# Linear attention and a gated MLP on one core: the second batch's keys loaded earlier and in pieces, the z products in quarters of the array, the last output in halves

## The chip, the cores and the metric

The kernel runs on one core of one Trainium2 chip. The metric is the device time of one execution in microseconds (us), the median of several runs. The core has TensorE (PE, its weight loads shown as PEld), VectorE (DVE), ScalarE (ACT), GpSimd (POOL) and SyncE (SP), which here only issues DMAs. SBUF has 128 partitions, and TensorE writes to PSUM.

## The reference

```python
def _attn_ref(q, k, v, S1, S2):          # q, k, v: 4 batches, 4 heads, 1088 rows, 32 columns; S1, S2: 8 x 32
    def phi(x):
        a = np.einsum('rd,bhsd->bhsr', S1, x)
        b = np.einsum('rd,bhsd->bhsr', S2, x)
        return np.einsum('bhsi,bhsj->bhsij', a, b).reshape(*x.shape[:-1], r * r)   # 64 features
    q_p, k_p = (phi(q), phi(k))
    kv = np.einsum('bhsf,bhsd->bhfd', k_p, v)
    z = np.sum(k_p, axis=2)
    num = np.einsum('bhsf,bhfd->bhsd', q_p, kv)
    den = np.einsum('bhsf,bhf->bhs', q_p, z)[..., None] + 1e-06
    return num / den

def _moe_ref(x, w_gate, w_val, w_out, rms_g):   # x: 4352 rows of 128; 128 x 1536, 128 x 1536, 1536 x 128
    xn = x / np.sqrt(np.mean(x * x, axis=-1, keepdims=True) + 1e-06) * rms_g
    g = xn @ w_gate
    return g * (1.0 / (1.0 + np.exp(-g))) * (xn @ w_val) @ w_out
```

The attention's output, with its heads side by side, is the input x of the gated MLP.

## The kernel before

**Tiling.** The 4352 rows are taken in nine chunks: eight of 512 columns and one of 256. The 1536 hidden columns are twelve slices j of 128. One pair of chunk and slice is a slot, 108 in all: three matmuls for the gate (`g_ps`), three for the value (`v_ps`), a Silu on ACT (`s`), a product on DVE (`h`), and one to three matmuls that add into `o_ps`. Three matmuls stand for one fp32 product, because operands are split into a rounded part and a rest (`w_hi`, `w_lo`, `x_hi`, `x_lo`, `h_hi`, `h_lo`). The first two chunks run slices 0 to 5 and then 6 to 11.

**Weights.** A slice arrives as raw double-precision words (`w_raw`, 384 KB). ACT takes the absolute value (`w_tmp`), DVE makes fp32 of it in four steps (L310, L315, L320, L324), ACT and POOL split it. This goes on until about 57 us, beside the first slots.

**Keys.** `kside` handles one batch of keys: a load of `kt` and of `vt` in pieces, matmuls with `s_t` (L482) that give both projections a and b, copies of these to `ab` by ACT (`bring`, L509), their outer product `phi`, then the sums over the rows. Batch 0 has its own path at the start. For batches 1 to 3 `kv_turned` forms kv by 36 small matmuls (L407) and z by nine products of a and b over 128 rows each (L401): a 64 x 32 result that holds all heads against all heads. ACT copies it to `gram`, and four matmuls with the constant `spread` and a mask `column` pick the wanted entries out of it.

**Queries.** `qside` divides by den, takes squares (`sq`), a root on POOL (`rstd`), scales (`xn`), transposes on TensorE (L764), and makes `x_hi` (ACT) and `x_lo` (DVE). For chunk 0 this is done for rows 0 to 255 and 256 to 511 apart; the first half's squares are DVE's and the second half's are ACT's.

**Order.** A planner (`Plan.run`) walks all tasks with assumed costs, keys (due times) and clocks for each engine, and writes each engine's instructions out in the order it finds; the engines then run them strictly in that order. Where it expects TensorE to idle early on, it puts in fillers (`keep_warm`, L292), matmuls of zeros into an `att` bank of PSUM. Every `keep_warm` is one matmul, and one fp32 matmul shows as two records in the trace. `att` has three banks; the fillers' tile holds one of them until the last filler. Keys of batch 1 go into two `att` banks (`ahead`) during the prologue, and TensorE can write such a bank only when its earlier reader is done. SP's loads take eight semaphores in turn, and each load waits for the landing of the one eight places ahead.

**What the change touches.** `K1` holds the four due times of batch 1's `kside` (its key matmuls, its outer products, its sums, its loads). The last slot's output is copied in two halves of 128 columns, by ACT and by DVE, into one tile `o_sb`, and goes out by one DMA of SP.

## Time and profile before

| | us |
|---|---|
| median of 3 runs (lowest to highest) | 270.78 (270.42 to 270.82) |
| the profiled execution's own time | 270.91 |
| its span, first to last instruction | 269.1 |
| busy: PE | 262.6 (98%) |
| busy: DVE | 189.5 (70%) |
| busy: ACT | 153.2 (57%) |
| busy: POOL | 66.7 (25%) |

The profiled execution took 270.91 us, of which 1.81 us lie outside the span. Times in the rows are counted from the span's start. A row of the timeline gives start, duration, engine, line, operation, what is written from what, count, and in brackets how long the engine was idle before and what released it. "issue" there means that no single cause shows.

### The profile page before, as it was taken

How to read it: one execution, taken by the hardware profiler on the slowest of the kernel's cores; microseconds unless marked ns; L12 is line 12 of the kernel's file. 1: busy time of each engine (PE TensorE's matmuls, PEld its weight loads, DVE VectorE, ACT ScalarE, POOL GpSimd, SP SyncE). 2: the span in 40 equal slices, each digit the busy share in tenths (PEclk: the TensorE clock that was granted, in tenths of full speed). 3: DMA queues.
4: the chain of work that ended last, by engine and by line, in shares of the span. 5: the costliest groups of instructions: out<-in, count | busy, mean ns of one | idle time of the engine just before them, and what ended most of it. 6: DMA issues, size and time to landing. Idle time of an engine off the chain costs nothing.

```text
span 269.1 us, 5080 instructions
## 1 busy us (share of the span) xinstructions
PE 262.6 (98%) x1899; PEld 208.9 (78%) x1899; DVE 189.5 (70%) x378; ACT 153.2 (57%) x319; POOL 66.7 (25%) x79
## 2 busy tenths in 40 slices
PE   8889999999999999999999999999999999999995
PEld 5758677677887878878887887788887888788894
DVE  5769999666847887677666795678568566766532
ACT  4457763675654544565556554565655565665662
POOL 3033751367350130001800220003300700100262
PEclk9979999999999999999999999999999999999999
DMA  6999500642521520035002500024002200100010
GB/s 202 363 388 371 181 2 0 200 110 58 130 67 48 153 57 2 1 100 131 26 0 80 148 11 2 0 85 130 4 0 68 61 0 0 40 2 0 0 41 21
DMA packets 12953, 22.11 MB, mean 82 GB/s; under 512 B 1664, under 2 KB 5760, under 8 KB 12928
## 3 DMA queue, kind: packets, MB, share of 16 engines
q1 hardware_dynamic: 12928, 21.78, 25.8%
q8 instruction: 15, 0.25, 0.4%
q14 instruction: 10, 0.08, 0.1%
HBM read 18.69 MB, written 3.08 MB: 81 GB/s over the span
## 4 chain that ended last, share of the span: by engine, by line
PE 96%; DMA 2%; issue 1%; SPq 0%; DVE 0%; ACT 0%
PE g_ps L822 27%; PE v_ps L822 27%; PE o_ps L853 23%; PE o_ps L840 4%; PE att L659 4%; DMA q<-qT 2%; PE att L764 2%; PE att L482 2%; PE att L401 1%; PE att L407 1%; PE att L675 1%; PE o_ps L531 1%; PE att L572 1%; PE att L292 1%; PE att L591 0%
## 5 line engine op out<-in xcount | busy, mean ns | idle before, releaser
L833 DVE TENSOR_TENSOR h<-v_ps,s 128x512 f32<-128x512 f32 (+2 forms) x109 | 71.1, 654 | 28.1 <-PE v_ps L822 12.1
L242 ACT CAST h_hi<-h 128x512 fp32r<-128x512 f32 (+1 forms) x91 | 54.2, 596 | 52.5 <-DVE h L833 52.3
L829 ACT ACTIVATE s<-g_ps 128x512 f32<-128x512 f32 (+1 forms) x108 | 62.0, 574 | 25.1 <-PE g_ps L822 22.5
L250 DVE TENSOR_TENSOR h_lo<-h,h_hi 128x512 fp32r<-128x512 f32 x74 | 53.0, 720 | 32.0 <-ACT h_hi L242 31.0
L822 PE MATMUL g_ps<-x_hi,w_hi 128*128 128x512 f32 (+1 forms) x110 | 46.0, 419 | 0.0
L822 PE MATMUL v_ps<-x_hi,w_hi 128*128 128x512 f32 (+1 forms) x110 | 42.2, 383 | 0.0
L822 PE MATMUL g_ps<-x_hi,w_lo 128*128 128x512 f32 (+1 forms) x110 | 42.0, 382 | 0.0
L822 PE MATMUL g_ps<-x_lo,w_hi 128*128 128x512 f32 (+1 forms) x110 | 41.7, 379 | 0.0
L822 PE MATMUL v_ps<-x_hi,w_lo 128*128 128x512 f32 (+1 forms) x110 | 41.5, 377 | 0.0
L822 PE MATMUL v_ps<-x_lo,w_hi 128*128 128x512 f32 (+1 forms) x110 | 41.4, 377 | 0.0
L757 POOL TENSOR_TENSOR rstd<-ms,mhalf 128x4 f32<-128x4 f32 (+1 forms) x10 | 9.5, 951 | 112.3 <-DVE ms L773 111.9
L853 PE MATMUL o_ps<-h_hi,w_lo 128*128 128x512 f32 (+1 forms) x94 | 36.1, 384 | 0.0
L853 PE MATMUL o_ps<-h_hi,w_hi 128*128 128x512 f32 (+1 forms) x94 | 36.1, 384 | 0.0
L853 PE MATMUL o_ps<-h_lo,w_hi 128*128 128x512 f32 (+1 forms) x94 | 36.0, 383 | 0.0
L249 POOL TENSOR_TENSOR h_lo<-h,h_hi 128x512 fp32r<-128x512 f32 (+1 forms) x20 | 20.4, 1029 | 30.7 <-ACT h_hi L242 30.6
L822 PEld LDWEIGHTS g_ps<-x_hi,w_hi 128*128 128x128 f32 x110 | 20.7, 188 | 6.5 <-issue 1.8
L822 PEld LDWEIGHTS g_ps<-x_hi,w_lo 128*128 128x128 f32 x110 | 20.7, 188 | 5.0 <-issue 1.7
L822 PEld LDWEIGHTS v_ps<-x_hi,w_hi 128*128 128x128 f32 x110 | 20.7, 188 | 4.6 <-DVE ms L773 0.2
L249 POOL TENSOR_TENSOR w_lo<-w_f,w_hi 128x256 fp32r<-128x256 f32 (+1 forms) x24 | 17.2, 734 | 28.2 <-ACT w_hi L242 28.1
L822 PEld LDWEIGHTS g_ps<-x_lo,w_hi 128*128 128x128 f32 x110 | 20.9, 190 | 4.2
L822 PEld LDWEIGHTS v_ps<-x_hi,w_lo 128*128 128x128 f32 x110 | 20.7, 188 | 4.1 <-issue 0.2
L822 PEld LDWEIGHTS v_ps<-x_lo,w_hi 128*128 128x128 f32 x110 | 20.6, 188 | 4.0
(104 smaller groups left out, 301.3 us busy)
## 6 DMA issues: line engine op xcount, KB each, us to landing
w_raw<-w SPq DMA_DIRECT2D x12, 384.0 KB
at<-far SPq DMA_DIRECT2D x12, 256.0 KB
bt<-far SPq DMA_DIRECT2D x24, 128.0 KB
q<-qT SPq DMA_DIRECT2D x8, 256.0 KB
outT<-o_sb SPq DMA_DIRECT2D x8, 256.0 KB
vt<-v SPq DMA_DIRECT2D x9, 204.0 KB
kt<-kT SPq DMA_DIRECT2D x9, 192.0 KB
far<-abt SPq DMA_DIRECT2D x12, 64.0 KB
```

Source lines behind the costliest of these rows:

```text
L242: "act": (n * 0.835 + 172, lambda: nc.scalar.copy(out=out(), in_=in_()), 0),
L249: "pool": (n * 2.1 + 150, lambda: nc.gpsimd.tensor_tensor(out=out(), in0=in_(), in1=hi(), op=ALU.subtract), 0),
L250: "dve": (n * 1.04 + 140, lambda: nc.vector.tensor_tensor(out=out(), in0=in_(), in1=hi(), op=ALU.subtract), penalty, True),
L482: nc.tensor.matmul(out=abv[hf * HALF:(hf + 1) * HALF, t - t0, :], lhsT=kt()[:, s0:s0 + HALF], rhs=sblk_t, start=True, stop=True)
L659: nc.tensor.matmul(out=nv[hf * HALF:(hf + 1) * HALF, t, p, :], lhsT=phiqs[c][1]()[:, p, l0:l0 + HALF], rhs=kvs[(STARTS[c] + l0) // S][:, p ...
L757: nc.gpsimd.tensor_tensor(out=rstd()[:, us, 0], in0=ms()[:, us], in1=mhalf[:, us], op=ALU.pow)
L764: nc.tensor.transpose(out=xt()[:, t * P:(t + 1) * P], in_=xn()[:, t, :], identity=ident)
L822: nc.tensor.matmul(out=acc()[:, cs], lhsT=wt[:, j, i3, :], rhs=x()[:, cs], start=(i == 0), stop=(i == 2))
L829: act(n, t + 0.3, lambda: nc.scalar.activation(out=s()[:, :n], in_=gps()[:, :n], func=AF.Silu), cols(gps, whole[0]), [s])
L833: lambda cs=cs: nc.vector.tensor_tensor(out=h()[:, cs], in0=vps()[:, cs], in1=s()[:, cs], op=ALU.mult),
L840: lambda cs=cs: nc.tensor.matmul(out=o_ps()[:, cs], lhsT=w_f[:, j, 2], rhs=h()[:, cs], start=first, stop=last and cs.stop == n),
L853: nc.tensor.matmul(out=o_ps()[:, :n], lhsT=wt[:, j, 2, :], rhs=x()[:, :n], start=first and i == 0, stop=last and i == 2,)
```

## The change

- `K1`'s load time goes from -26.5 to -28.2, and batch 1's values get load times of their own, `VT1` = (-15, -14, -13). On SP's queue the three key pieces then stand ahead of the second weight slice, and the three value pieces behind the eighth.
- The keys of a batch in `ahead` (batch 1) become three planner tasks, one for each piece of three tiles of 128 rows, where one task waited for all three pieces. ACT's three copies wait for their own piece.
- z's nine products (L401): the 64-column operand that held both a and b becomes a's 32 columns, and the product of tile t goes to quarter t % 4 of the output's partitions. The four quarters are summed later by the matmuls with `spread`, which now has 128 rows in place of 64; `gram` is 128 x 32. For this `ab` is laid out with all of a ahead of all of b.
- `spread` and `column` are made on POOL by six instructions, ahead of the four memsets of `kv`, where DVE made them by five. The planner's clock for POOL starts at 5200 in place of 2200.
- The last output's halves have tiles of their own (`o_end0`, `o_end1`), and each goes out by its own DMA: ACT's half on ACT's queue, DVE's half on SP's.

```diff
-K1 = -41,9,10,-26.5
+K1 = -41,9,10,-28.2
+VT1 = (-15, -14, -13)
...
-    spread = const.tile([NB, H, F], F32, name="spread")
-    for h in range(H):
-        nc.vector.tensor_copy(
...
-    nc.vector.tensor_reduce(out=column, in_=ident.rearrange("p (o j) -> p j o", j=R), axis=AX.X, op=ALU.add)
+    spread = const.tile([P, H, F], F32, name="spread")
+    column = const.tile([P, 4 * R], F32, name="column")
+
+    def patterns():
+        nc.gpsimd.tensor_tensor(out=column, in0=ident[:, :4 * R], in1=ident[:, 4 * R:8 * R], op=ALU.add)
+        for k in (2, 3):
+            nc.gpsimd.tensor_tensor(out=column, in0=column, in1=ident[:, 4 * k * R:4 * (k + 1) * R], op=ALU.add)
+        nc.gpsimd.tensor_copy(
+            out=spread.rearrange("p h (i j) -> p (h i) j", j=R), in_=column.unsqueeze(2).to_broadcast([P, H * R, R])
+        )
+        for k in (2, 1):
+            nc.gpsimd.tensor_tensor(out=column[:, :k * R], in0=column[:, :k * R], in1=column[:, k * R:2 * k * R], op=ALU.add)
+
+    patterns()
...
             for t in range(KT):
-                ab = abs_[t // 3]()[:, t % 3]
-                nc.tensor.matmul(
-                    out=tr()[:NB, :H * R], lhsT=ab.rearrange("p h c r -> p (h c r)"), rhs=ab[:, :, 1, :], start=(t == 0), stop=(t == KT - 1)
-                )
+                a, b = (abs_[t // 3]()[:, c, t % 3].rearrange("p h r -> p (h r)") for c in range(2))
+                rows = slice(t % 4 * H * R, (t % 4 + 1) * H * R)
+                nc.tensor.matmul(out=tr()[rows, :H * R], lhsT=a, rhs=b, start=(t < 4), stop=(t >= KT - 4), skip_group_check=True)
...
-        act(H * R, key, lambda: nc.scalar.copy(out=gram(), in_=tr()[:NB, :H * R]), [tr], [gram])
+        act(H * R, key, lambda: nc.scalar.copy(out=gram(), in_=tr()[:, :H * R]), [tr], [gram])
...
-    ktl, vtl = early if first else ([early] * 3, (early + 0.5, early + 2, early + 2))
+    ktl, vtl = early if first else ([early] * 3, (early + 0.5, early + 2, early + 2) if b > 1 else VT1)
...
-        abs_ = [sb("ab", [P, 3, H, 2, R], 3) for _ in groups]
+        abs_ = [sb("ab", [P, 2, 3, H, R], 3) for _ in groups]
...
-        if not first:
+        if b in ahead:
+            for g, (lo, hi) in enumerate(pieces):
+                pe(453, kab, lambda lo=lo, hi=hi, g=g: mm(lo, hi, banks[g // 2], g // 2 * 6), [(kt, g), "sblk"], [(banks[g // 2], g)], True)
+        elif not first:
             pe(151 * KT, kab, mms, [(kt, g) for g in range(3)] + ["sblk"], banks, True)
...
+        if not left:
+            for i, cs in enumerate(rest_of):
+                o_end, wd = sb(f"o_end{i}", [P, P], 1), cs.stop - cs.start
+                if i:
+                    dve(wd * 1.04, t + 1.0, lambda cs=cs, o=o_end: nc.vector.tensor_copy(out=o(), in_=o_ps()[:, cs]), done, [o_end])
+                else:
+                    act(wd, t + 1.0, lambda cs=cs, o=o_end: nc.scalar.copy(out=o(), in_=o_ps()[:, cs]), done, [o_end])
+                load(
+                    wd * P * 4, t, lambda cs=cs, o=o_end, on=nc.sync if i else nc.scalar: on.dma_start(
+                        out=out[:, s0 + cs.start:s0 + cs.stop], in_=o()
+                    ), [("out", c, i)], [o_end],
+                )
+            return
...
-    plan.run({"pe": PE0, "act": 1900, "dve": 1000, "pool": 2200, "dma": 600}, keep_warm, SLOW, URGENT, WINDOW)
+    plan.run({"pe": PE0, "act": 1900, "dve": 1000, "pool": 5200, "dma": 600}, keep_warm, SLOW, URGENT, WINDOW)
```

The planner moves instructions that the diff does not name. The line numbers grow by seven to ten in the prologue's tasks, so L482, L292, L764, L822, L330, L739, L509, L787 and L780 of before are L489, L300, L774, L832, L338, L749, L519, L797 and L790 of the changed kernel.

SP's queue in the prologue, from the gain vector on, before: kt are keys (192 KB a piece), vt values, w_raw weight slices, q queries.

```order
L884 DMA gain_t<-gain 128x1
L383 DMA w_raw<-w 128x768
L465 DMA kt<-kT 128x384 x3
L383 DMA w_raw<-w 128x768
L468 DMA vt<-v 128x408
L552 DMA q<-qT 128x512
L468 DMA vt<-v 128x408 x2
L383 DMA w_raw<-w 128x768 x2
```

The same stretch now:

```order
L901 DMA gain_t<-gain 128x1
L472 DMA kt<-kT 128x384 x3
L391 DMA w_raw<-w 128x768 x2
L562 DMA q<-qT 128x512
L391 DMA w_raw<-w 128x768 x2
L562 DMA q<-qT 128x512
```

The second weight slice stands behind the three key pieces, and the value pieces have left the stretch.

ACT's order in the prologue, from the second half of chunk 0's phi (phiq) to x_hi of the first half, before. The first w_tmp row is slice 1's, the second slice 2's; sq are the squares of the second half of chunk 0's rows; the three ab rows are batch 1's.

```order
L605 COPY phiq_228<-v_ps_234 128x2x256
L330 ACTIVATE w_tmp_255<-w_raw_184 128x384
L242 CAST w_hi_98<-w_f_100 128x256
L242 CAST w_hi_98<-w_f_100 128x128
L330 ACTIVATE w_tmp_309<-w_raw_232 128x384
L739 ACTIVATE sq_317,ss_318<-x_274 128x128 x2
L509 COPY ab_324<-att_281 128x192
L509 COPY ab_328<-att_281 128x192
L509 COPY ab_335<-att_294 128x192
L787 ACTIVATE x_hi_340<-att_332,gain_t_97 128x256
```

The same stretch now:

```order
L615 COPY phiq_230<-v_ps_235 128x2x256
L243 CAST w_hi_99<-w_f_101 128x256
L243 CAST w_hi_99<-w_f_101 128x128
L338 ACTIVATE w_tmp_289<-w_raw_214 128x384
L519 COPY ab_302<-att_271 128x12x2x8
L519 COPY ab_309<-att_271 128x12x2x8
L519 COPY ab_318<-att_294 128x12x2x8
L338 ACTIVATE w_tmp_323<-w_raw_233 128x384
L749 ACTIVATE sq_327,ss_328<-x_280 128x128 x2
L797 ACTIVATE x_hi_344<-att_338,gain_t_98 128x256
```

The three copies of batch 1's keys and slice 2's w_tmp have moved ahead of the squares.

TensorE from batch 1's keys to the first matmuls of slot 0, before:

```order
L482 MATMUL att<-s_t,kt 64x64 x18
L292 MATMUL att<-const-float32-0.0 1x128 x2
L764 MATMUL att<-ident,xn 128x128 x2
L292 MATMUL att<-const-float32-0.0 1x128 x2
L764 MATMUL att<-ident,xn 128x128 x2
L572 MATMUL att<-s_t,q 128x64 x2
L822 MATMUL g_ps<-x_hi,w_hi 128x256
```

The same stretch now:

```order
L489 MATMUL att<-s_t,kt 64x64 x18
L300 MATMUL att<-const-float32-0.0 1x128 x5
L774 MATMUL att<-ident,xn 128x128 x2
L300 MATMUL att<-const-float32-0.0 1x128 x2
L832 MATMUL g_ps<-x_hi,w_hi 128x256
```

Five fillers stand between the keys and the first transposes in place of two, and the first half's gate matmuls (three, of which the last row is the first) have moved ahead of the second half's transposes. The order of the 108 slots behind it is the same.

More of the change, by code (lines that the diff above doesn't have):

```diff
@@ L259, in attention_then_glu @@
     nc.vector.memset(ones, 1.0)
-    spread = const.tile([NB, H, F], F32, name="spread")
-    for h in range(H):
-        nc.vector.tensor_copy(
-            out=spread[:, h].rearrange("p (i j) -> p i j", j=R),
-            in_=ident[:NB, 2 * h * R:(2 * h + 1) * R].unsqueeze(2).to_broadcast([NB, R, R]),
-        )
-    column = const.tile([P, R], F32, name="column")
-    nc.vector.tensor_reduce(out=column, in_=ident.rearrange("p (o j) -> p j o", j=R), axis=AX.X, op=ALU.add)
+    spread = const.tile([P, H, F], F32, name="spread")
[6 more added lines that the diff above has]
+            out=spread.rearrange("p h (i j) -> p (h i) j", j=R), in_=column.unsqueeze(2).to_broadcast([P, H * R, R])
+        )
+        for k in (2, 1):
+            nc.gpsimd.tensor_tensor(out=column[:, :k * R], in0=column[:, :k * R], in1=column[:, k * R:2 * k * R], op=ALU.add)
+    patterns()
     zeros = nc.const_aps.tensor(0.0, [P, P], F32)
@@ L395, in kv_turned @@
         acc, tr = ps("att", 3), ps("att", 3)
-        both, gram, picked = sb("kv_both", [P, 2, F], 1), sb("gram", [NB, H * R], 1), sb("picked", [P, 2, R], 1)
+        both, gram, picked = sb("kv_both", [P, 2, F], 1), sb("gram", [P, H * R], 1), sb("picked", [P, 2, R], 1)
         def kvmm():
             for t in range(KT):
-                ab = abs_[t // 3]()[:, t % 3]
-                nc.tensor.matmul(
-                    out=tr()[:NB, :H * R], lhsT=ab.rearrange("p h c r -> p (h c r)"), rhs=ab[:, :, 1, :], start=(t == 0), stop=(t == KT - 1)
-                )
+                a, b = (abs_[t // 3]()[:, c, t % 3].rearrange("p h r -> p (h r)") for c in range(2))
+                rows = slice(t % 4 * H * R, (t % 4 + 1) * H * R)
+                nc.tensor.matmul(out=tr()[rows, :H * R], lhsT=a, rhs=b, start=(t < 4), stop=(t >= KT - 4), skip_group_check=True)
             for t in range(KT):
@@ L412, in kv_turned @@
         pe(
-            1450, key, kvmm, [(phis[g], g) for g in range(3)] + [(vt, g) for g in range(3)] + [(abs_[g], g) for g in range(3)],
+            1330, key, kvmm, [(phis[g], g) for g in range(3)] + [(vt, g) for g in range(3)] + [(abs_[g], g) for g in range(3)],
             [acc, tr], True,
         )
-        act(H * R, key, lambda: nc.scalar.copy(out=gram(), in_=tr()[:NB, :H * R]), [tr], [gram])
+        act(H * R, key, lambda: nc.scalar.copy(out=gram(), in_=tr()[:, :H * R]), [tr], [gram])
         act(
@@ L437, in kv_turned @@
             17, key, lambda: nc.vector.tensor_tensor(
-                out=picked(), in0=sums(), in1=column.unsqueeze(1).to_broadcast([P, 2, R]), op=ALU.mult
+                out=picked(), in0=sums(), in1=column[:, :R].unsqueeze(1).to_broadcast([P, 2, R]), op=ALU.mult
             ), [tr], [picked],
@@ L498, in outer @@
             def outer(eng, ab=ab, phi=phi, ts=ts, m=m, near=near, ab_ps=ab_ps, o=o):
-                both = ab()[:, ts].rearrange("p t h c r -> p (t h) c r")
+                both = ab()[:, :, ts].rearrange("p c t h r -> p (t h) c r")
                 a = ab_ps()[:, o:o + m * HALF].rearrange("p (th c r) -> p th c r", c=2, r=R) if near else both
@@ L509, in bring @@
                 nc.scalar.copy(
-                    out=ab()[:, ts].rearrange("p t h c r -> p (t h) c r")[:, :, c0:],
+                    out=ab()[:, :, ts].rearrange("p c t h r -> p (t h) c r")[:, :, c0:],
                     in_=ab_ps()[:, o:o + m * HALF].rearrange("p (th c r) -> p th c r", c=2, r=R)[:, :, c0:],
@@ L515, in kside @@
                 pe(151 * m, kab, lambda lo=lo, hi=hi, ab_ps=ab_ps: mm(lo, hi, ab_ps, lo), [(kt, g), "sblk"], [ab_ps], True)
-            act(HALF * m // (2 if first and near else 1), kab, bring, [ab_ps], [(ab, i)])
+            act(HALF * m // (2 if first and near else 1), kab, bring, [(ab_ps, g) if b in ahead else ab_ps], [(ab, i)])
             if near or b in SBD:
@@ L873, in slot @@
         else:
-            for i, cs in enumerate(rest_of):
-                if i:
-                    dve(
-                        (cs.stop - cs.start) * 1.04, t + 1.0,
-                        lambda cs=cs: nc.vector.tensor_copy(out=o_sb()[:, cs], in_=o_ps()[:, cs]), done, cols(o_sb, cs),
-                    )
-                else:
-                    act(cs.stop - cs.start, t + 1.0, lambda cs=cs: nc.scalar.copy(out=o_sb()[:, cs], in_=o_ps()[:, cs]), done, cols(o_sb, cs))
+            act(n, t + 1.0, lambda: nc.scalar.copy(out=o_sb()[:, :n], in_=o_ps()[:, :n]), done, cols(o_sb, whole[0]))
         load(n * P * 4, t, lambda: nc.sync.dma_start(out=out[:, s0:s0 + n], in_=o_sb()[:, :n]), [("out", c)], cols(o_sb, whole[0]))
```

## Prediction

> **What bounds the kernel now.** I read the page's busy times and the chain that ended last, then the stretches of the prologue, then its timeline, since the change touches three places: the prologue, the z products and the last output.
>
> ```profile
> PE 262.6 (98%) x1899; PEld 208.9 (78%) x1899; DVE 189.5 (70%) x378; ACT 153.2 (57%) x319; POOL 66.7 (25%) x79
> ...
> PE 96%; DMA 2%; issue 1%; SPq 0%; DVE 0%; ACT 0%
> ```
>
> TensorE is busy for 98% of the span and makes 96% of the chain. So microseconds taken from TensorE's own work after the prologue count in full, and work of other engines counts only where TensorE waits for it. That is in the prologue:
>
> ```profile
> 12.20:15.60 3.40, 1.64 (x47) 1.42 (x46) 3.16 (x14) 1.66 (x6) 1.44 (x2) 1.00 1.05 392
> 15.60:19.00 3.40, 3.40 (x24) 1.66 (x21) 1.49 (x5) 2.13 (x10) 1.17 (x2) 0.51 1.01 383
> ```
>
> The columns are length, busy time of PE, PEld, DVE, ACT and POOL with counts, TensorE's granted clock, DMA share and GB/s. From 12.2 to 15.6 us TensorE works 1.64 of 3.40 us; from 15.6 to 19.0 it has about half its clock (0.51). Between 19.46, the first row of slot 0, and the tail I find no wait in its timeline.
>
> ```profile
> 11.81 1.84 SPq L383 DMA_DIRECT2D w_raw<-w  x2
> ...
> 13.39 0.43 DVE L715 TENSOR_TENSOR x<-att,rden 128x256 f32<-128x256 f32 x1
> ...
> 13.77 0.36 SPq L552 DMA_DIRECT2D q<-qT  x1
> ...
> 13.92 0.92 PE L482 MATMUL att<-s_t,kt 128*64 128x64 f32 x24 [1.20 <-issue]
> ...
> 14.51 0.55 ACT L330 ACTIVATE w_tmp<-w_raw 128x384 f32<-128x384 f32 x1 [0.95 <-DMA w_raw<-w]
> ...
> 14.88 0.42 DVE L715 TENSOR_TENSOR x<-att,rden 128x256 f32<-128x256 f32 x1
> ...
> 15.22 0.35 DVE L310 TENSOR_SCALAR w_tmp<-w_tmp 128x384 f32<-128x384 f32 x1
> ...
> 15.34 0.31 ACT L739 ACTIVATE sq<-x 128x128 f32<-128x128 f32 x1 [0.28 <-DVE x L715]
> ...
> 15.40 0.73 PE L482 MATMUL att<-s_t,kt 128*64 128x64 f32 x12 [0.57 <-PE att L482]
> ...
> 15.94 0.74 ACT L509 COPY ab<-att 128x192 f32<-128x192 f32 x3
> ...
> 16.06 1.01 PE L292 MATMUL att<-const-float32-0.0 128*1 128x128 f32 x4
> ...
> 16.31 0.74 POOL L757 TENSOR_TENSOR rstd<-ms,mhalf 128x2 f32<-128x2 f32 x1 [0.99 <-DVE ms L773]
> ...
> 17.01 0.69 PE L764 MATMUL att<-ident,xn 128*128 128x128 f32 x2
> ...
> 17.73 0.47 ACT L787 ACTIVATE x_hi<-att,gain_t 128x256 fp32r<-128x256 f32 x1 [1.06 <-PE att L764]
> 18.10 0.68 ACT L780 ACTIVATE xn<-x,rstd 128x128 f32<-128x128 f32 x2
> 18.24 0.48 DVE L767 SCALAR_TENSOR_TENSOR x_lo<-att,gain_t,x_hi 128x256 fp32r<-128x256 f32 x1 [1.75 <-ACT x_hi L787]
> ...
> 19.46 0.37 PE L822 MATMUL g_ps<-x_hi,w_hi 128*128 128x256 f32 x1
> ...
> 19.97 0.48 DVE L767 SCALAR_TENSOR_TENSOR x_lo<-att,gain_t,x_hi 128x256 fp32r<-128x256 f32 x1
> ```
>
> **Keys loaded earlier: nothing.** The key matmuls start at 13.92, 0.10 us after DVE ends x (13.39 + 0.43 = 13.82), and go on at 15.40, 0.10 after the second x (15.30). These x read the `att` banks into which the keys go: with one bank held by the fillers' tile, only two are left. The keys had landed: the two weight loads at 11.81 to 13.65 and the query load at 13.77 stand eight places behind the three key pieces and waited for them. So the transfer taken forward is not what TensorE waits for. DVE's order up to both x is unchanged but for the patterns (below), so 13.92 and 15.40 stay.
>
> **The second weight slice later: nothing.** It swaps places with the key pieces, so it lands at the latest when the third of them did, 13.77. ACT's w_tmp takes 0.55 and DVE's next step on it starts at 15.22: 0.9 us of cover. Without it, x_lo behind that DVE step would be late by what is missing. The values are needed only by the kv products, quoted below, long after slot 0's start, and the later slices land earlier.
>
> **ACT's new order and five fillers: 0 to 1.4 us lost, 1.1 taken.** Before, the key matmuls end about 16.1, two fillers (four records) take 16.06 to 17.01, 0.24 a record, and the transposes of the first half follow. Now ten records follow: 16.06 + 10 x 0.24 = 18.43 at half clock, 1.42 late. The chain behind it is x_hi 0.72 later (19.15), x_lo 0.51 after that (19.66), then DVE's same three weight steps, and x_lo of the second half 1.73 after the first (21.39 to 21.87, before 20.45). ACT's side comes in time for that: its third key copy waits for the keys (about 16.15), then a copy of 0.25, w_tmp of 0.55 and squares of 0.60 (15.34 to 15.94) end near 17.5 instead of 15.94; rstd then ends near 18.5 instead of 17.05, ahead of x_hi at 19.15. So the squares' delay of 1.5 us hides under the fillers. If the fillers ran at full clock, half the time each, they would end at 16.06 + 1.2 = 17.3 and x_hi would wait for the squares at 17.5: no later than 17.73. The lower end is therefore 0, the upper 1.4. I take 1.1, near the row's half clock, less something because the slow stretch need not fall on all ten records in each run. [...]
>
> **z in quarters: 2.6 us gained.** The z products and the kv products of one batch, and the same pair later, in the chain:
>
> ```profile
> 44.31 1.17 PE att L401 x18
> 45.47 1.14 PE att L407 x72
> ...
> 101.05 1.17 PE att L401 x18
> 102.21 1.14 PE att L407 x72
> ...
> 160.08 1.16 PE att L401 x18
> 161.25 1.14 PE att L407 x72
> ```
>
> L401 has 18 records in 1.17 us, 65 ns each: a 64-column operand, always at the same columns of the array. L407 has 72 in 1.14, 16 ns each: 32 columns, in turn on four quarters. The changed products have L407's shape, with 32 moving columns instead of 64, and the same turn. At 16 ns they take 18 x 0.016 = 0.29, so 0.88 less, and I take 0.86, three times: 2.6. The other end: the key matmuls, two halves of the array in turn, have 24 records in 0.92 us, 38 ns, which gives 0.69 and a gain of 0.48, 1.4 in all. L407 is the nearer row. With the change of shape between L401 and L407 gone, up to 0.1 more each. [...]
>
> `spread` with 128 rows instead of 64, and ACT's copy of 128 instead of 64 partitions: eight records and one copy as before, so nothing; ends -0.1 and +0.1 for all three. ACT's key copies now write in strides: no row has that at this size, so 0 to 0.1.
>
> **Patterns on POOL: nothing.**
>
> ```profile
> 1.25 0.66 POOL L273 MEMSET kv<- 128x132 f32 x4
> ...
> 2.66 0.20 DVE L338 TENSOR_SCALAR s_low<-s_raw 128x64 uint32<-128x64 uint32 x1 [0.25 <-DMA s_raw<-sw]
> ...
> 5.80 1.07 POOL L501 TENSOR_TENSOR phi<-ab 128x512 f32<-128x512 f32 x1 [3.89 <-ACT ab L509]
> ...
> 7.76 1.59 PE L531 MATMUL o_ps<-vt,phi 128*64 128x34 f32 x48
> ```
>
> DVE loses five instructions but then waits for s_raw until 2.66, so it gains nothing. POOL idles 3.89 us ahead of phi, which TensorE reads in the second third of L531's row, about 8.3, 1.4 us after phi's end at 6.87. So 5.3 us are covered.
>
> ```profile
> L249 POOL TENSOR_TENSOR w_lo<-w_f,w_hi 128x256 fp32r<-128x256 f32 x12 | 10.7, 893 | 24.9 <-ACT w_hi L242 24.9
> ...
> L249 POOL TENSOR_TENSOR w_lo<-w_f,w_hi 128x128 fp32r<-128x128 f32 x12 | 6.9, 574 | 3.3 <-ACT w_hi L242 3.2
> ```
>
> Five small sums at no more than 0.57 and one copy of 256 columns at no more than 0.89 are 3.8 us. Above 5.3 each further microsecond would be one of the whole.
>
> **The last output: 0.3 us gained.**
>
> ```profile
> 265.81 0.27 ACT L881 COPY o_sb<-o_ps 128x128 f32<-128x128 f32 x1 [1.34 <-PE o_ps L840]
> 266.11 0.29 DVE L878 COPY o_sb<-o_ps 128x128 f32<-128x128 f32 x1 [1.06 <-ACT o_sb L881]
> 266.43 0.33 SPq L882 DMA_DIRECT2D outT<-o_sb  x1
> ```
>
> DVE's copy waits for ACT's, and the DMA for both. With tiles apart both copies can start at 265.81, and both DMAs issue near 266.13: 0.30 less. A first DMA on ACT's queue has no row; SP's issues took 0.33 here and 1.84 for two above, so between -0.3 and +0.3.
>
> **Sum.** 270.91 - 2.6 - 0.3 + 1.1 = 269.1 for the profiled execution. It lies 0.13 above the median of 270.78, so against the runs shown: 269.0.
>
> **Rivals.** First, the fillers cost nothing, because the slow stretch falls elsewhere: 270.78 - 2.9 = 267.9. For it speaks that the fillers then end before the squares do; against it the 0.51 of the row that covers them. Second, the quarters overlap only as the halves of the key matmuls do, 38 ns: 270.78 - 1.4 - 0.3 + 1.1 = 270.2. Third, on the other side: the z products stay at 65 ns each, because the spacing comes from issuing and not from the array. Then nothing pays for the prologue: 270.78 - 0.3 + 1.1 = 271.6. It decides from about 50 ns a record, where the gain of 3 x 18 x 15 ns = 0.8 only pays the rest. L407's 16 ns is against it. Fourth, the slow stretch lasts for another 3.4 us, since the idle time ahead of it is as before and more of it is filled with zeros: half of 3.4, 1.7 us more, 270.7, no change. Against it: the two stretches above, where full work in one was followed by full clock at 19.46.
>
> **How the numbers follow.** Forecast 0.60, first rival 0.18, second 0.09, third 0.07, fourth 0.06. A measurement of this kernel can tell about 0.2%, 0.54 us, from no change: faster means below 270.24. Faster are the forecast, the first rival and half of the second: 0.60 + 0.18 + 0.045, rounded to 0.82. Same are the fourth and the other half: 0.11. Slower is the third: 0.07. The range from 267.8 to 270.4 holds the forecast, the first rival and most of the second; the forecast alone, with the prologue between 0.6 and 1.4 and the tail between 0 and 0.35, lies within 268.4 to 269.6.
>
> **What would show it.** z: eighteen records of L410 in about 0.3 us, and L414 straight behind. Prologue: the keys (L489) still at 13.9 and 15.4, ten filler records behind them, the first transposes (L774) near 18.4 instead of 17.0, squares (L749) near 16.9, the last gate rows of slot 0 near 22 instead of 20.5. Patterns: phi on POOL still near 5.8. Tail: both copies at once, the DMAs 0.3 us behind the first. The forecast is wrong if L410 keeps more than 40 ns a record, if the half clock misses the fillers or stays past 19.5, or if TensorE waits anywhere behind slot 0.

## The result, and the profile after

The changed kernel takes 267.69 us (median of 4 runs, 267.10 to 267.80), the kernel before 270.60 in the same comparison (median of 4, 270.20 to 270.82): a ratio of 0.989, interval 0.987 to 0.9909. That is 1.1% faster, and just below the range of the prediction. Timed again beside other kernels, the changed kernel took 267.78 (6 runs, 267.49 to 269.45) against 270.15 (11 runs, 269.85 to 271.06): 0.9922, interval 0.9899 to 0.9945. Why the two ratios differ is part of what follows.

The profiled execution took 267.65 us, with a span of 265.9 (before 269.1). From its page, and from its view by stretches, the rows that answer to those of before:

```profile
PE 260.1 (98%) x1905; PEld 206.6 (78%) x1905; DVE 189.9 (71%) x373; ACT 153.0 (58%) x319; POOL 68.4 (26%) x85
```

```profile
12.20:15.60 3.40, 1.63 (x48) 1.41 (x46) 3.16 (x14) 1.59 (x5) 1.44 (x2) 1.00 1.02 402
15.60:19.00 3.40, 3.35 (x29) 1.95 (x25) 1.65 (x5) 2.47 (x9) 1.16 (x2) 1.00 1.03 408
```

TensorE is idle for as long as before in the first stretch (busy 1.63 of 3.40 us), but the second one, which had a clock of 0.51, now has 1.00. This is the first surprise. The timeline of the prologue shows what that did:

```profile
13.79 0.92 PE L489 MATMUL att<-s_t,kt 128*64 128x64 f32 x24 [1.20 <-issue]
...
15.29 0.57 PE L489 MATMUL att<-s_t,kt 128*64 128x64 f32 x12 [0.58 <-PE att L489]
...
15.79 1.27 PE L300 MATMUL att<-const-float32-0.0 128*1 128x128 f32 x10
...
16.61 0.30 ACT L749 ACTIVATE sq<-x 128x128 f32<-128x128 f32 x1
...
16.99 0.44 PE L774 MATMUL att<-ident,xn 128*128 128x128 f32 x2
...
17.46 0.47 ACT L797 ACTIVATE x_hi<-att,gain_t 128x256 fp32r<-128x256 f32 x1 [0.17 <-PE att L774]
```

The keys start at 13.79 and 15.29, ten filler records follow, and ScalarE's squares come at 16.6: all close to the forecast. But the ten records take 1.27 us and not 2.4, so the first transposes stand at 16.99 (before 17.01) and not at 18.4.

The z products and what stands around them, in TensorE's timeline before and after (L675 and L685 are the first instruction behind the pair of z and kv products):

```profile
44.24 1.24 PE L401 MATMUL att<-ab 128*64 128x32 f32 x18
45.40 1.21 PE L407 MATMUL att<-phi,vt 128*32 128x64 f32 x72
46.54 0.66 PE L675 MATMUL att<-q,sab 128*64 128x128 f32 x8
```

```profile
44.28 0.34 PE L410 MATMUL att<-ab 128*32 128x32 f32 x17
44.43 0.26 PE L414 MATMUL att<-phi,vt 128*32 128x64 f32 x3
44.46 0.20 PE L410 MATMUL att<-ab 128*32 128x32 f32 x1
44.49 1.17 PE L414 MATMUL att<-phi,vt 128*32 128x64 f32 x69
45.59 0.66 PE L685 MATMUL att<-q,sab 128*64 128x128 f32 x8
```

The pair starts 0.04 us later than before (so the new prologue as a whole gained nothing in these two executions, although only the one before has a half-clock stretch) and takes 45.59 - 44.28 = 1.31 us instead of 46.54 - 44.24 = 2.30. The other two pairs gain the same. The kv products' first row stands 0.15 behind the first z product: 17 of the 18 records have started by then, the last starts 0.03 later.

The tail, its last products before, and then what the changed kernel has:

```profile
264.73 1.04 PE L840 MATMUL o_ps<-h,w_f 128*128 128x256 f32 x6
```

```profile
261.73 1.04 PE L850 MATMUL o_ps<-h,w_f 128*128 128x256 f32 x6
262.81 0.27 ACT L883 COPY o_end<-o_ps 128x128 f32<-128x128 f32 x1 [1.32 <-PE o_ps L850]
263.10 0.37 ACTq L885 DMA_DIRECT2D outT<-o_end  x1
263.10 0.29 DVE L881 COPY o_end<-o_ps 128x128 f32<-128x128 f32 x1 [1.04 <-ACT o_end L883]
263.42 0.33 SPq L885 DMA_DIRECT2D outT<-o_end  x1
```

From the end of the last product (262.77) to the end of the span (265.87) it is 3.10 us, before 265.77 to 269.10, 3.33: 0.23 gained. But VectorE's copy still waits for ScalarE's, although the tiles they write are now apart, so the last DMA is issued no earlier: 0.65 behind the last product, before 0.66 (the prediction has that row, 266.43). What is shorter is the time from that issue to the end of the span, 2.45 instead of 2.67; that DMA now carries one half instead of both.

So from profile to profile: three pairs at 0.99 to 1.00, 3.0; the tail 0.23; the prologue 0. That is the 3.2 us between the two spans.

### The profile page after: what moved, and what is told of

It reads as the page before. It is cut to its first block, busy times and chain, and to the rows that moved or that the text cites. A ratio compares the mean times of both kernels' runs of the same rounds, so it can differ in the third digit from the quotient of the medians.

```text
span 265.9 us, 5091 instructions
## 1 busy us (share of the span) xinstructions
PE 260.1 (98%) x1905; PEld 206.6 (78%) x1905; DVE 189.9 (71%) x373; ACT 153.0 (58%) x319; POOL 68.4 (26%) x85
## 4 chain that ended last, share of the span: by engine, by line
PE 98%; issue 1%; DVE 0%; ACT 0%
PE g_ps L832 28%; PE v_ps L832 27%; PE o_ps L863 23%; PE o_ps L850 4%; PE att L669 4%; PE att L300 2%; PE att L774 2%; PE att L489 1%; PE att L414 1%; PE att L685 1%; PE o_ps L541 1%; PE att L582 1%; PE g_ps L489 0%; PE att L601 0%; PE v_ps L489 0%
## 5 line engine op out<-in xcount | busy, mean ns | idle before, releaser
L832 PE MATMUL g_ps<-x_hi,w_hi 128*128 128x512 f32 (+1 forms) x110 | 46.1, 419 | 0.0
L832 PE MATMUL v_ps<-x_hi,w_hi 128*128 128x512 f32 (+1 forms) x110 | 42.3, 384 | 0.0
L832 PE MATMUL g_ps<-x_hi,w_lo 128*128 128x512 f32 (+1 forms) x110 | 42.0, 381 | 0.0
L832 PE MATMUL g_ps<-x_lo,w_hi 128*128 128x512 f32 (+1 forms) x110 | 41.7, 379 | 0.0
L832 PE MATMUL v_ps<-x_lo,w_hi 128*128 128x512 f32 (+1 forms) x110 | 41.5, 378 | 0.0
L832 PE MATMUL v_ps<-x_hi,w_lo 128*128 128x512 f32 (+1 forms) x110 | 41.5, 377 | 0.0
L832 PEld LDWEIGHTS g_ps<-x_hi,w_hi 128*128 128x128 f32 x110 | 20.7, 188 | 6.8 <-issue 1.8
L832 PEld LDWEIGHTS g_ps<-x_hi,w_lo 128*128 128x128 f32 x110 | 20.7, 188 | 5.0 <-issue 1.7
L832 PEld LDWEIGHTS g_ps<-x_lo,w_hi 128*128 128x128 f32 x110 | 20.9, 190 | 4.6 <-DVE x_lo L777 0.4
L832 PEld LDWEIGHTS v_ps<-x_hi,w_hi 128*128 128x128 f32 x110 | 20.7, 188 | 4.6 <-DVE ms L783 0.2
L832 PEld LDWEIGHTS v_ps<-x_hi,w_lo 128*128 128x128 f32 x110 | 20.7, 188 | 4.1 <-issue 0.2
L832 PEld LDWEIGHTS v_ps<-x_lo,w_hi 128*128 128x128 f32 x110 | 20.7, 188 | 4.1
```

The source lines that it names most:

```text
L832: nc.tensor.matmul(out=acc()[:, cs], lhsT=wt[:, j, i3, :], rhs=x()[:, cs], start=(i == 0), stop=(i == 2))
```

## The experiments

All kernels, with the time from the first of the second batch's key products (13.79 above) to the first z product (44.28 above), which measures the prologue by itself:

| kernel | median us (range, runs) | ratio to before, interval | keys to z, us | least busy window of TensorE, clock in the next |
|---|---|---|---|---|
| before | 270.2, 270.42, 270.15 (beside three groups of the others) | 1 | 30.32 | 49%, half |
| changed | 267.69 (267.10-267.80, 4) | 0.989, 0.987-0.9909 | 30.49 | 70%, full |
| z alone | 266.78 (266.64-267.47, 4) | 0.9871, 0.9846-0.9896 | 29.60 | 64%, full |
| keys alone | 270.96 (270.66-271.68, 12) | 1.0032, 1.0017-1.0046 | 30.44 | 68%, full |
| no fillers | 268.71 (267.31-270.04, 11) | 0.9947, 0.9922-0.9971 | 31.46 | 48%, half (two windows) |
| gap filled | 269.86 (269.61-270.31, 11) | 0.9986, 0.9971-1.0 | 29.60 | 77%, full |
| copies late | 267.37 (266.99-268.70, 6) | 0.9881, 0.9842-0.992 | 30.18 | 70%, full |
| z and gap | 266.95 (266.77-267.18, 6) | 0.9859, 0.982-0.9899 | 29.58 | 81%, full |
| runs of quarters | 267.76 (267.43-269.10, 7) | 0.9899, 0.9866-0.9932 | 31.31 | 48%, half |
| changed again | 267.78 (267.49-269.45, 6) | 0.9922, 0.9899-0.9945 | 31.45 | 48%, half |
| all mended | 266.71 (266.45-266.77, 4) | 0.9866, 0.9849-0.9883 | 29.61 | 75%, full |
| halves | 268.55 (1) | - | 29.58 | 68%, full |
| six in a quarter | 268.02 (1) | - | 30.48 | 60%, full |
| two banks | 266.55 (1) | - | 29.58 | 77%, full |

The last two columns are from each kernel's profiled execution. In these traces the granted clock changes only at steps of 3.413 us (in the kernel before, half clock from 15.66 to 19.07), at another phase in each execution (an edge falls at 12.24 there, at 13.59 in the changed kernel); the windows are cut there, and the share is TensorE's busy time in the emptiest one between 7 and 20 us. The record also has the mean granted clock of every run beside the profiled ones. Where a profile shows one half-clock window in the prologue, this mean is 0.992 to 0.994, with two 0.987, and without 0.998 to 1.000 (a window that starts behind the last product takes off up to 0.002). So a run of 0.994 or less had a half-clock window, and one of 0.997 or more had none.

**One part at a time.** First z in quarters alone (with the patterns on POOL that it needs):

```diff
-K1 = -41,9,10,-28.2          # of the changed kernel; keys, fillers and tail
+K1 = -41,9,10,-26.5          # as in the kernel before, z and patterns as changed
...
```

> The kernel before with the products for z in quarters (and the two patterns on POOL that they need) as the only change; keys, fillers and last output as before. Theory A (the whole gain is z, about 0.98 us for each of three pairs; the clock is a matter of how busy each free-running 3.4 us window is, so the prologue of before with its two idle stretches still gives a half-clock stretch): 270.6 - 2.95 = about 267.7, half clock in one window of the prologue. Rival B (z is worth the 2.6 us that was predicted and the new prologue the rest): 268.0 or more. Rival C (the patterns moved off DVE shift the start of the window, and the clock is full here too): 267.7 less 0.6 to 1.1, so 266.6 to 267.1, and then the keys and fillers of the changed kernel cost time.

Measured: 266.78, below the changed kernel's 267.69. The pair takes 44.35 - 43.03 = 1.32 us, and the clock was full:

```profile
43.03 0.34 PE L409 MATMUL att<-ab 128*32 128x32 f32 x17
...
44.35 0.66 PE L681 MATMUL att<-q,sab 128*64 128x128 f32 x8
```

So z is worth 1.0 a pair without the new prologue, against rival B, and what stands beside it in the changed kernel costs time: keys to z takes 29.60 here and 30.49 there. Theory A's 267.7 and its half-clock stretch did not come; all four runs had a clock of 0.997 or more. The time is rival C's, but C's reason, that the patterns shift the window, is not shown: the windows start elsewhere in each execution, and in this one the emptiest, from 10.53 to 13.94, was busy for 64%.

Then the keys in three tasks, with their five fillers, alone on the kernel before:

```diff
-K1 = -41,9,10,-26.5
+K1 = -41,9,10,-28.2
+VT1 = (-15, -14, -13)
+        if b in ahead:
+            for g, (lo, hi) in enumerate(pieces):
+                pe(453, kab, lambda lo=lo, hi=hi, g=g: mm(lo, hi, banks[g // 2], g // 2 * 6), [(kt, g), "sblk"], ...
...
```

> The kernel before with the keys in three tasks ahead of the second weight slice, with the five fillers that this brings, as the only change. Theory A: the order itself is worth about nothing or costs a little, and what is measured is the clock: 270.4 to 270.8 with the clock full all through, about 1 us more with a half-clock stretch. Rival B (the prologue is a gain of its own, hidden in the comparison of before and after by something else): 270.0 or less.

Measured: 270.96, 0.32% slower (0.17 to 0.46%), with the clock full in its profile and 0.999 or more in all 12 runs. The new order is a loss, more of one than "about nothing": at full clock the keys-to-z time is 30.44 here and 29.60 where the old order runs at full clock (next), a difference of 0.84 us. ScalarE's timeline has one reason:

```profile
14.77 0.54 ACT L513 COPY ab<-att 128x192 f32<-128x192 f32 x2 [0.92 <-PE att L483]
15.91 0.32 ACT L513 COPY ab<-att 128x192 f32<-128x192 f32 x1 [0.60 <-PE att L483]
...
16.57 0.30 ACT L743 ACTIVATE sq<-x 128x128 f32<-128x128 f32 x1
```

The squares wait in ScalarE's queue behind the third copy, which waits for the keys. In the old order they start 1.28 us earlier:

```profile
15.29 0.31 ACT L741 ACTIVATE sq<-x 128x128 f32<-128x128 f32 x1 [0.41 <-DVE x L717]
...
15.89 0.74 ACT L511 COPY ab<-att 128x192 f32<-128x192 f32 x3
```

**The clock.** Those rows are of the kernel before with four fillers in the 1.2 us in which TensorE waits for the keys (`keep_warm(k)` issues k filler matmuls, not one):

```diff
         def mms():
+            if b in ahead:
+                keep_warm(4)()
             mm(0, 6, banks[0], 0)
```

> The kernel before with four fillers (0.96 us) put into the 1.2 us idle stretch of TensorE ahead of the second batch's key products, as the only change. Theory A: the window from 12.24 to 15.66 us rises from 49% busy to 75%, the half-clock stretch from 15.66 to 19.07 us is gone, and the time falls by 0.6 to 1.1 us to 269.5 to 270.0. Rival F (the clock follows a single idle stretch of a certain length, and 0.55 us between the key products is enough for it): the half-clock stretch stays, 270.6. Rival G (what ends last in that stretch is not TensorE): the stretch goes and the time stays, 270.6.

Measured: 269.86, and all 11 runs lie within 0.7 us, where the 28 runs of the kernel before beside it reach from 269.53 to 271.76. Its profile has the full clock throughout, and keys to z take 29.60 us instead of 30.32: the half-clock stretch cost 0.72.

```profile
13.87 0.92 PE L482 MATMUL att<-s_t,kt 128*64 128x64 f32 x24 [0.22 <-issue]
...
43.47 1.24 PE L401 MATMUL att<-ab 128*64 128x32 f32 x18
```

The median fell by only 0.34, less than expected, because most runs of the kernel before have no such stretch: by their granted clocks 5 of the 28 had one (270.44 to 271.76, median 270.74) and 23 had none (269.53 to 271.13, median 269.94). Its profiled execution, at 270.91, was one of the rarer kind. Against the 23 the fillers cost nothing that the runs can tell. The clock is not the whole spread: in the profiled executions the first of the second batch's key products starts anywhere from 13.43 (z alone) to 14.31 us (copies late), both at full clock; why was not followed.

The opposite, the changed kernel without its five fillers:

```diff
-            for _ in range(k):
+            for _ in range(0 if k == 5 else k):
```

> The changed kernel with the five fillers between the keys and the first turn of x left out. Theory A (a window that is less than about half busy is followed by one at half clock): the window from 13.6 to 17.0 us falls from about 80% busy to about 42%, the next one is at half clock, and the time is up by 0.5 to 1.2 us, 268.2 to 268.9. Rival D (the fillers hold up the turns of x and keep nothing up): the first turn starts 0.3 us earlier or more, the clock stays full, 267.3 to 267.6. Rival E (they lie wholly beside the wait for DVE's squares): same start, clock full, 267.7.

Measured: 268.71, with runs from 267.31 to 270.04. By their granted clocks six of the 11 had two half-clock windows (268.71 to 270.04), one had one (268.39) and four had none (267.31 to 268.43). That is theory A's price; the four lie about 267.7, where the changed kernel's full-clock runs lie, so they show no gain of rival D. The profiled one had two windows at half clock. Each row is one 3.413 us window; columns as above, clock third from the right:

```profile
12.05:15.47 3.42, 1.65 (x44) 1.43 (x43) 3.18 (x13) 1.59 (x5) 1.44 (x2) 1.00 1.01 399
15.47:18.88 3.41, 3.12 (x21) 1.98 (x21) 1.54 (x6) 1.78 (x9) 0.84 (x2) 0.50 1.03 411
18.88:22.29 3.41, 3.41 (x16) 3.02 (x16) 2.81 (x7) 2.34 (x8) 1.75 (x3) 0.50 0.80 250
22.29:25.70 3.41, 3.41 (x39) 3.24 (x40) 3.20 (x8) 2.93 (x8) 0.85 (x2) 1.00 0.76 227
```

The kernel before, whose window at half clock has an emptier one ahead of it, too, and behind it the changed kernel when it ran once more:

```profile
12.24:15.66 3.42, 1.66 (x49) 1.44 (x47) 3.18 (x14) 1.68 (x7) 1.44 (x2) 1.00 1.03 386
15.66:19.07 3.41, 3.41 (x23) 1.67 (x19) 1.50 (x5) 2.07 (x9) 1.17 (x2) 0.50 1.02 384
```

> The changed kernel once more, as the measure for the one beside it: 267.4 to 267.9.

The changed kernel's two windows, and TensorE's timeline behind its keys:

```profile
12.59:16.00 3.41, 1.64 (x45) 1.35 (x40) 3.17 (x13) 1.59 (x5) 1.44 (x2) 1.00 1.04 407
16.00:19.42 3.42, 3.42 (x17) 1.70 (x16) 0.43 (x3) 1.85 (x8) 1.16 (x2) 0.50 1.03 406
```

```profile
15.96 2.29 PE L300 MATMUL att<-const-float32-0.0 128*1 128x128 f32 x10
18.18 0.69 PE L774 MATMUL att<-ident,xn 128*128 128x128 f32 x2
```

The median is 267.78, but the 2 of the 6 runs with a clock of 0.994 took 268.80 and 269.45 (the other four 267.49 to 267.81), and the first of these, the profiled one, is close to the forecast of 269.0: ten fillers at 0.23 each, the first transposes at 18.18, keys to z 31.45. In the first profile of the changed kernel the same idle stretches were cut by a window's edge at 13.59:

```profile
10.18:13.59 3.41, 2.38 (x52) 1.87 (x48) 3.04 (x9) 1.56 (x5) 0.28 (x1) 1.00 1.04 410
13.59:17.00 3.41, 2.63 (x47) 2.04 (x47) 2.10 (x10) 1.88 (x8) 1.16 (x2) 1.00 1.03 412
```

Over all kernels, the four windows of the prologue that were busy for 48 or 49% were each followed by half clock, and all windows of 60% and more, at full clock, by full clock. The ends of the traces narrow this: whole windows of 27 to 40% (five kernels) were followed by half clock, but one of 54% (z alone, 259.70 to 263.11 us, busy for 1.84 of 3.41) by full clock. Theory A fits every window at full clock; in these traces the limit lies between 49 and 54%. Rival F does not fit: the changed kernel has the same two idle stretches in both its profiles, and the half clock in one.

An estimate from these rows says how often it happens. In the kernel before the two idle stretches reach from 12.72 to 15.40 us, 2.68 us, so both fall into one window of 3.413 for 0.73 of 3.413 us of its possible starts: about one execution in five. By the granted clocks, it was 14 of the 54 runs of the kernel before, and 4 of 36 with the new order and its five fillers (changed, keys alone, copies late, and runs of quarters and six in a quarter below). With fillers in the gap it was none of 22 (gap filled, z and gap, all mended, two banks).

**What the order behind the keys costs.** The changed kernel, with ScalarE's copies made to come after its squares:

```diff
-            act(..., bring, [(ab_ps, g) if b in ahead else ab_ps], [(ab, i)])
+            act(..., bring, [(ab_ps, g), (of_first["ss"], 2), (of_first["ss"], 3)] if b in ahead else [ab_ps], [(ab, i)])
...
```

> The changed kernel with ScalarE's three copies of the second batch's keys put behind its squares of the first x (in the changed kernel the copies and a weight step stand ahead of the squares and wait for the keys); the five fillers stay. Theory H (the new prologue costs 0.8 us at full clock because the squares, and through them the second half of x, wait behind the copies; the fillers hold the first half up by 0.5): squares at 14.8 to 15.5 instead of 16.6 to 17.3, the second turns of x near 18.3 instead of 18.8, and 0.3 to 0.5 us less than the changed kernel: 267.2 to 267.4 against 267.7. Rival I (the five fillers alone cost it): no change, 267.7. Rival J (the copies alone cost it): the full 0.8, 266.9.

Measured: 267.37, and keys to z 30.18, 0.31 less than the changed kernel's 30.49 and 0.58 more than the old order at full clock. Theory H, in its own sizes: about 0.3 from the squares behind the copies, the other 0.58 from five fillers instead of two, which occupy TensorE past the time at which the first half of x is ready (xn of that half ends at 16.30, the fillers run from 16.30, and the first transposes start at 17.50; the profile of all mended, below, has two and is at 29.61). This split holds in this order only: with the squares still late, leaving the fillers out gained nothing in the four full-clock runs above.

With both mended, or without the new key order at all:

```diff
# z and gap: z alone, and
         def mms():
+            if b in ahead:
+                keep_warm(4)()
# all mended: copies late, and four fillers ahead of the first key piece, two behind the third
+            if not g:
+                keep_warm(4)()
             mm(lo, hi, banks[g // 2], g // 2 * 6)
-            for _ in range(k):
+            for _ in range(2 if k == 5 else k):
```

> Only z in quarters (with its patterns on POOL) on the kernel before, and four fillers in the 1.2 us idle stretch ahead of the second batch's keys; keys, their copies and the last output as before. Theory A: full clock whatever the phase of the 3.4 us windows, 266.4 to 266.9, with a spread of a few tenths, and 0.8 to 1.2 below the changed kernel. Rival C (z alone was at full clock for another reason, and fillers only cost): above 267.0.

> The changed kernel with four fillers ahead of the second batch's keys, two instead of five behind them, and ScalarE's key copies behind its squares. If the order behind the keys costs the changed kernel 0.86 us (0.3 from the squares behind the copies, 0.5 to 0.6 from the fillers) and the gap fillers only keep the clock, this is 0.8 us below the changed kernel in the same call: 266.6 to 267.0, and as fast as z with gap fillers (266.95) or 0.1 better by the halved last output. If the keys in three pieces cost something by themselves, it stays above 267.2.

Measured: 266.95 and 266.71, with keys to z of 29.58 and 29.61. All four runs of the second lie below all six of the changed kernel beside it, by 1.07 us from median to median (267.78; 0.98 from that of its four full-clock runs), and its ratio of 0.9866 is below the changed kernel's 0.9922 with intervals apart. It has the lowest median of the kernels that leave nothing out, but it is not told apart from z and gap (0.9859) or z alone (0.9871), whose intervals overlap with its own. The keys in pieces cost nothing by themselves, and gain nothing either; what they pulled along cost.

**What sets the spacing of the z products.** Three forms: the old 64 columns in turn on the two halves of the array; 32 columns, with runs of 3, 2, 2 and 2 products in a quarter; 32 columns, with six in one quarter.

```diff
+                rows = slice(t % 2 * NB, (t % 2 + 1) * NB)                  # halves, on the kernel before
+                quarter = t * 4 // KT                                       # runs of quarters, on the changed kernel
+                quarter = max(0, t - 5)                                     # six in a quarter, on the changed kernel
```

> The kernel before with its z products, 64 columns wide as they are, put in turn into the lower and the upper half of the array's columns; only the lower half's sum is used, so half of the z products is left out of the result. Theory Q (products follow each other closely when they turn over parts of the array): the spacing falls from 65 ns a record towards the 38 of the key products, which do the same, and each group of 18 from 1.17 to about 0.69 us. Rival W (the spacing is that of the width of 64): it stays at 65 ns and 1.17 us.

> The changed kernel with the nine products given to the quarters in runs of three, two, two and two instead of in turn; same result. Theory Q (a product waits only for the one ahead of it in its own quarter, about 130 ns a product): five of the nine steps stay in their quarter, 5 x 110 ns = 0.55 us more for each of three pairs, 269.2 to 269.5. Rival W (width alone): 267.6 to 267.9.

> The changed kernel with the first six of the nine products in one quarter and one in each other; same result. Theory Q: five steps in a row within a quarter at about 110 ns more each, 0.5 us more for the group. Rival W, which the runs of three and two favour (18 records in 0.2 us): 0.2 to 0.25 us for the 18 records.

TensorE's timeline from the first z product to the first kv product, in the same order:

```profile
43.33 0.77 PE L402 MATMUL att<-ab 128*64 128x32 f32 x18
44.03 1.21 PE L409 MATMUL att<-phi,vt 128*32 128x64 f32 x72
```

```profile
45.57 0.40 PE L411 MATMUL att<-ab 128*32 128x32 f32 x16
45.78 0.22 PE L415 MATMUL att<-phi,vt 128*32 128x64 f32 x1
45.79 0.21 PE L411 MATMUL att<-ab 128*32 128x32 f32 x2
```

```profile
44.06 0.54 PE L411 MATMUL att<-ab 128*32 128x32 f32 x17
44.42 0.22 PE L415 MATMUL att<-phi,vt 128*32 128x64 f32 x1
```

From the first z product to the first kv product, for 18 records: 1.16 us with 64 columns in one place (44.24 to 45.40 above), 0.70 in turn on two halves, 0.36 with six of nine in one quarter, 0.21 in runs, 0.15 in turn on four quarters. That is about 64, 39, 20, 12 and 8 ns a record; in the three forms with quarters the last one or two records start up to 0.03 behind the first kv product, so these are a little low. The whole pairs (2.30, 1.84, 1.50, 1.37 and 1.31 us) differ by the same amounts within 0.02. The halves came out as theory Q said. For the quarters neither theory holds alone: even six in a row are far quicker than 64 columns in one place, and still 0.21 slower than in turn. Five steps within a quarter cost 0.06 in short runs and 0.21 in a long one, so it is not a fixed wait for the product ahead; what it is stays open. For all nine in one quarter there is no result.

**The tail.** All mended, with the second half's last product in another PSUM tile, from which VectorE copies; each copy now also waits for its own half alone, where both waited for the whole:

```diff
+                own = apart if not left and cs.start else None             # apart: a tile of g_ps
-                        out=o_ps()[:, cs], lhsT=w_f[:, j, 2], rhs=h()[:, cs], start=first, ...
+                        out=(own or o_ps)()[:, cs], lhsT=w_f[:, j, 2], rhs=h()[:, cs], start=first or own is not None, ...
...
-                    dve(wd * 1.04, t + 1.0, lambda cs=cs, o=o_end: nc.vector.tensor_copy(out=o(), in_=o_ps()[:, cs]), done, [o_end])
+                    dve(wd * 1.04, t + 1.0, lambda cs=cs, o=o_end: nc.vector.tensor_copy(out=o(), in_=apart()[:, cs]), cols(apart, cs), [o_end])
...
```

> The mended kernel, with the very last product of the second half of the last output written into another PSUM tile, from which VectorE copies it (that half lacks the sum of the earlier products). Theory K (VectorE's copy waits for ScalarE's because both read the same PSUM tile): both copies start together, the two output DMAs issue within 0.1 us of each other, and from the first copy to the end of the span it takes 0.3 us less than in the mended kernel. Rival L (the second DMA or its queue sets the end): VectorE's copy starts earlier and the span ends as before.

The end of its timeline:

```profile
261.58 0.39 PE L858 MATMUL g_ps<-h,w_f 128*128 128x128 f32 x2
261.78 0.27 ACT L891 COPY o_end<-o_ps 128x128 f32<-128x128 f32 x1 [1.11 <-PE o_ps L858]
262.01 0.29 DVE L889 COPY o_end<-g_ps 128x128 f32<-128x128 f32 x1 [0.76 <-PE g_ps L858]
262.08 0.37 ACTq L893 DMA_DIRECT2D outT<-o_end  x1
262.33 0.33 SPq L893 DMA_DIRECT2D outT<-o_end  x1
```

VectorE's copy now waits for TensorE alone and starts at 262.01, ahead of the end of ScalarE's at 262.05: that much of theory K is shown. From the end of the last product, 261.97, to the end of the span, 264.77, it is 2.8 us, against 3.1 in the mended kernel. That is not K's price alone, since ScalarE's half no longer waits for the second product either and starts 0.19 ahead of that product's end instead of 0.04 behind it. An estimate from the rows: had VectorE's copy still come 0.03 behind ScalarE's, as in the mended kernel, it would have started at 262.08, so about 0.07 of the 0.3 needed K. From the first copy on, the time of which K's 0.3 was said, it is 2.99 us against 3.07 (261.82 to 264.89 in the mended kernel). The two DMA issues are 0.25 apart rather than the 0.1 expected, because ScalarE's half is ready earlier. A form with tiles apart in which both copies wait for both products was not run.

## Why the prediction was wrong

The sign was right; the time was 1.3 us too high: 0.9 from the prologue and 0.4 from z. The first rival, at 267.9 with a chance of 0.18, was right that the slow stretch falls elsewhere, and wrong that the fillers then cost nothing; that its time is near is luck, since z's extra 0.4 and the stretch that the kernel before had in its own time made up for their cost. By its steps:

- **The fillers and ScalarE's new order, +1.1: the step that failed.** It took the half-clock stretch of one profiled execution as a fixture of the prologue, laid it over the new fillers and priced ten records at 0.24. The price was right: where the stretch falls on them, keys to z take 31.45 against 30.32, 1.13 more. But that is the rarer case: 2 of the changed kernel's 10 runs, by their granted clocks. In the other eight no window was empty enough (in the profiled one the idle stretches fall into two windows), and then the order costs 0.89 (30.49 against 29.60) against a kernel before that is also at full clock, or 0.17 against the one that was profiled, which had the stretch. So the term was 0.17 and not 1.1 in the two executions profiled. The step's lower end, 0, compared unlike things: x_hi of the first half at full clock, 17.46 as it argued, with 17.73 of an execution at half clock; in the old order at full clock it starts at 16.94. Nor do the squares hide under the fillers at full clock: of the 0.89, 0.3 is the squares behind the copies, which the prediction saw ("1.5 us") and held to be covered. A half clock that misses the fillers is one of the prediction's own signs of being wrong.
- **The windows.** They are 3.413 us long in these traces, and one that was busy for 48 or 49% was enough for half clock in the next. The prediction had the rows of one execution, 1.64 of 3.40 us busy and then a clock of 0.51; what it needed was that the windows begin at another phase in each execution (at 12.24 and 15.66 us in the kernel before, at 13.59 and 17.00 in the changed kernel, at 12.59 and 16.00 when it ran once more), which by itself made the place of the stretch a matter of the run. The fillers did run at full clock in most runs (8 of 10), the case of the step's lower end, but because of where a window's edge fell.
- **z, -2.6: mechanism right, size short by 0.4.** The term was 0.86 a pair; it measured 0.99 to 1.00, three times. L407's 16 ns a record, with 64 moving columns, was taken over unchanged; with 32 moving columns, in turn on the four quarters, it is about 8. The other end, the key products' 38 ns, was right for what it was, halves of the array: 39.
- **The tail, -0.3: 0.23**, near by luck, and not for the reason given. Tiles apart do not let the copies start together; what they share is the PSUM tile that they read. Where both read one tile, VectorE's copy starts 0.02 us behind the end of ScalarE's (263.10 against 263.08, changed kernel); where they read two, 0.04 ahead of it (262.01 against 262.05, two banks). What makes the one wait no run shows. The last DMA was issued no earlier (0.65 behind the last product, before 0.66) and carries half as much; that this is the whole 0.23 fits the rows and was not tested apart.
- **The keys and the second weight slice, nothing: right.** 13.79 and 15.29, 0.1 us earlier than before, as DVE's x above them.
- **The patterns on POOL, nothing: right for phi**, at 5.88 against 5.80 (see the last section for DVE).

At full clock the sum closes: 269.86 (the kernel before with its gap filled) - 3.0 - 0.23 + 0.89 = 267.5, measured 267.7 (the changed kernel's eight full-clock runs). Against the executions with a half-clock window it would be 270.9 - 3.0 - 0.23 + 1.13 = 268.8, which is what the changed kernel's profiled run with such a window took, and the forecast but for the size of z. All runs of the changed kernel in the first ratio, 0.989, had the full clock (0.999 or 1.000). The clocks of the runs of before beside them are not on record; by their times three of the four (270.42, 270.78, 270.82) probably had a half-clock window, since only 5 of the 40 full-clock runs of before elsewhere lie above 270.4. In the second ratio, 0.9922, both kinds are on both sides: 3 of 11 and 2 of 6.

## What to carry to other kernels

When a profile shows a half-clock stretch, look up the window ahead of it and how busy it was (48 or 49% here), and forecast with and without the stretch: one execution tells its price (0.72 us in the kernel before), not its place (14 of that kernel's 54 runs had it). Where an idle wait of TensorE cannot be removed, fill that wait itself rather than the work behind it; here four fillers in the gap kept all 11 runs at full clock at no cost that they show, and three more behind it cost 0.6 us. The small products gained here from being narrow and from taking turns over the quarters (64 ns a record with 64 columns in one place, 20 with 32 columns and six of nine in one quarter, 8 in turn), even though they sum to one result, which a later product adds up.

## What the runs showed of the hardware

Two things beyond the windows were not expected. After a window at half clock the next was at full clock when that window was busy throughout (the four cases of 100%: before, changed again, runs of quarters, and the second half-clock window without fillers), but in the kernel without fillers one that was busy for 3.12 of 3.41 us at half clock was followed by a second at half clock. There is one such case, so where the limit lies is open.

And a 64-column VectorE step took 0.83 us instead of 0.20 while POOL's new patterns and its memsets ran. VectorE before, VectorE after, and POOL after:

```profile
3.25 0.20 DVE L347 TENSOR_SCALAR s_tmp<-s_tmp 128x64 uint32<-128x64 uint32 x1
```

```profile
3.22 0.83 DVE L355 TENSOR_SCALAR s_tmp<-s_tmp 128x64 uint32<-128x64 uint32 x1
```

```profile
2.83 0.59 POOL L274 TENSOR_TENSOR column<-column 128x16 f32<-128x16 f32 x2
3.36 0.65 POOL L281 MEMSET kv<- 128x132 f32 x4
```

It ended at 4.05, with POOL's last memset at 4.01. The other traces show it both ways. With the patterns on POOL the step takes 0.83 or 0.84 us in six traces, 0.70 in z and gap, 0.41 in z alone, and only 0.19 and 0.20 in six in a quarter and two banks; in these last two it is POOL that is late, with 0.65 us for its last two `column` sums in place of 0.59 and its memsets at 3.43 and 3.42 in place of 3.36. With the patterns on VectorE it takes 0.20 in all four traces. So in each of the ten executions with the patterns on POOL one of the two is late, and which one differs; that it waits for the other would fit these rows, and no run shows it. The key products of the first batch then started 0.1 us later than before (4.37 against 4.28), so little came of it.
